# One weight load split by partitions, TensorE's two gaps filled, and a table touched early, in a decode step on one core

## The chip, the cores and the metric

The kernel runs on one core of one Trainium2 chip. The metric is the device time of one execution in microseconds, the median of several runs. The core has five engines with instruction streams of their own: TensorE (PE) for matrix products, VectorE (DVE), ScalarE (ACT), GpSimd (POOL) and SyncE (SP), which here does nothing but issue loads. Data moves between HBM and the on-chip memory (SBUF) on 16 DMA engines; a DMA that is issued once is cut into packets, and each DMA engine that takes part writes the DMA's semaphore when its own share has landed (a completion write below). Matrix products land in PSUM, eight banks of 512 fp32 values in 128 partitions.

## The reference

One decode step of a transformer block for four sequences, all tensors bf16: attention over a cached sequence of 8192 positions with 32 heads of 128, then a gated MLP.

```python
B, Sq, D = 4, 1, 512;  H, Sk, Dh = 32, 8192, 128;  F = 1792
x = A_x
q = layernorm(x) @ wq                       # per head, D x (H*Dh)
p = softmax(q . k_cache * Dh**-0.5)         # per sequence and head, 8192 scores
h = x + concat_heads(p . v_cache) @ wo
g, u = layernorm(h) @ w_gate, layernorm(h) @ w_up
out = h + (sigmoid(g) * u) @ w_down
```

The two caches are 268 MB each; everything else is about 14 MB. Every byte is read once.

## The kernel before, in words

**Units.** The 128 pairs of sequence and head are worked on four at a time: `NU` = 32 units. A unit's K (8.4 MB) and V (8.4 MB) are one load each, 64 KB in each of 128 partitions. Three slots of SBUF hold them: K alternates between slots 0 and 1, V lives in slot 2, and the last V goes to slot 0 in two halves (`vh0`, `vh1`). SP issues all loads in the order of `order`: K of the next unit, V of this one, and so on.

**A unit's work.** `unit(u)` writes, for each engine, K's 16 chunks (`k_chunk`: DVE transposes a chunk, L320, and TensorE multiplies it with the query window `Lq`, L329), then the maxima and the exponentials (`maxima`, L336 to L343), then the P times V of the unit before (`pv(u - 1)`, L368, with the fold of its four strips, L377 and L381, and `extract`, L386 and L387), then the transposed weights `PTz` of this unit (`weights`, L349). Each engine runs its list in that order; a wait on a semaphore stands in front of an operation only where data comes from another engine. Units 1 to 31 are one loop on TensorE, and after it come, outside any loop, the last unit's P times V, in two halves of 32 matmuls that wait for `vh0` and `vh1`, and its fold and extraction.

**The tail.** ACT touches the square root's table while it has nothing else (L424). TensorE multiplies the collected outputs `OT` with wo (L431, 32 matmuls in two groups of 16, each with its own half of wo) on top of x, which has been in the same bank since the start. `layernorm` (L266 to L280) normalises the sum h: statistics on DVE, a square root on ACT, the row on DVE, four small transposing matmuls into bank `XS`, a copy. ACT then copies h to SBUF (L438). TensorE multiplies with w_gate (16 matmuls) and w_up (16 matmuls, the first 12 with the first up load and the last 4 with the second), both at L446, four at a time in four strips of columns. ACT takes the sigmoid of the gate (L457), DVE multiplies and transposes in two halves (L463, L466), TensorE multiplies with w_down in 14 pairs (L471), DVE adds h (L477), and SP and ACT store half of the result each (L514).

**Loads of the tail.** When K's last chunk has been transposed, SP issues wo in two loads (L501), w_gate (L503), w_up in two loads (L507; `WUC` cuts it into three quarters and one quarter of each partition's rows), and w_down in four (L512; `WDT`). They use the slots that K and V leave. All go through SP's one queue, in this order, behind the last V halves.

**Tokens.** `prog.token(key, by)` names a count of the semaphore `key`; `prog.dma` attaches 16 to it per DMA; a wait is for the count in the token. `emit(engine, f, waits)` appends an operation to an engine's list.

Of the kernel before, what the change touches and what calls it, by code (L numbers as in the profile page):

```python
# [7 lines left out]
FP32 = mybir.dt.float32  # L8
ALU = mybir.AluOpType
ACT = mybir.ActivationFunctionType  # L10
# [3 lines left out]
class _Prog:  # L14
# [60 lines left out]
    def emit(self, eng, fn, waits=(), incs=1, ch=None):  # L75
        todo = self._waits(eng, waits)
        key = ch or eng
        tok = self.token(key, incs) if incs else None
        self._put(eng, todo, key, fn, incs, 1)
        return tok  # L80
# [40 lines left out]
def bass_sequential_preLN__mha_block_cached__glu_gated_glu__decode_kernel(  # L121
# [13 lines left out]
    _, H, S, DH = A_k_cache.shape  # L135
    F = B_w_gate.shape[1]
    assert DH == 128 and H == 32 and D == 512 and F % 128 == 0 and B == 4 and S == 8192
    NC = D // 128
# [3 lines left out]
    NU = B * H // HU  # L142
# [9 lines left out]
    WUC = (0, 3, 4)  # L152
# [3 lines left out]
    prog = _Prog({"p2d": "dve", "d2d": "dve", "a2d": "dve", "d2p": "pe", "a2p": "pe",  # L156
                  "d2a": "act", "p2a": "act",
                  "k0": "dve", "k1": "dve", "v2": "pe"})
    emit = prog.emit

    with ExitStack() as es:
        def SB(name, shape, dt):
            return es.enter_context(nc.sbuf_tensor(name, shape, dt))

        def raw(t):
            return t.tensor if hasattr(t, "tensor") else t
# [3 lines left out]
        Lq = SB("Lq", [128, 528], BF16)  # L170
# [4 lines left out]
        mask = SB("mask", [128, 8], BF16)  # L175
# [5 lines left out]
        negm = SB("negm", [128, 32], FP32)  # L181
        rsb = SB("rsb", [128, 32], FP32)
        ident = SB("ident", [128, 16], BF16)
        dummy = SB("dumm", [128, 2], FP32)
        eps = SB("eps", [128, 1], FP32)

        kTb = kT[:, :].bitcast(BF16)
# [11 lines left out]
        def reg(slot, off, size):  # L199
            return KV[:, slot * SLOT + off:slot * SLOT + off + size]  # L200
# [14 lines left out]
        bank = [PS[:, 512 * i:512 * (i + 1)] for i in range(8)]  # L215
        SBK, OBK, EX, XS, XO, QB, DN = 0, 1, 2, 3, 4, (5, 6), 7
# [12 lines left out]
        t_wg = prog.token("wg", 16)  # L229
        t_wu = [prog.token(f"wu{i}", 16) for i in range(len(WUC) - 1)]  # L230
        t_vh = [prog.token(f"vh{i}", 16) for i in range(2)]
        t_wd = [prog.token(f"wd{i}", 16) for i in range(len(WDT) - 1)]

        t_eps = emit("pool", lambda e: e.memset(eps[:, :], EPS))
# [24 lines left out]
        for b in (OBK, EX, *QB, DN):  # L259
            t_ps0 = emit("act", lambda e, b=b: e.activation(bank[b], bass.AP(raw(Lq), 0, [[528, 128], [0, 512]]), ACT.Copy), [t_lq0])  # L260

        def cols(t, c):
            return t[:, c:c + NC * (B - 1) + 1:NC]

        def layernorm(src, waits, dst):
            a = emit("dve", lambda e: e.bn_stats(bst, src), waits)  # L266
            a = emit("dve", lambda e: e.bn_aggr(agg, bst), [a])
            a = emit("act", lambda e: e.activation(std[:, 0:1], agg[:, 1:2], ACT.Sqrt, bias=eps[0:B, :]), [a, t_eps])
            a = emit("dve", lambda e: e.reciprocal(std[:, 1:2], std[:, 0:1]), [a])
            t_row = emit("dve", lambda e: e.tensor_scalar(  # L270
                row, src, agg[:, 0:1], std[:, 1:2], op0=ALU.subtract, op1=ALU.mult), [a])

            def f(e):
                ins = None
                for c in range(NC):
                    ins = e.matmul(cols(bank[XS], c), row[:, c:c + NC * 127 + 1:NC], ident[0:B, 0:B],
                                   start=(c == 0), stop=(c == NC - 1), skip_group_check=True)
                return ins
            a = emit("pe", f, [t_row, t_ident])
            return t_row, emit("dve", lambda e: e.tensor_copy(dst, bank[XS][:, 0:NC * B]), [a])  # L280
# [4 lines left out]
        _, t_xn = layernorm(x_bf, [t_x], xnT)  # L285

        t_qr = []
        for g in range(2):
            def f(e, g=g):
                made = []  # L290
                for c in range(NC):
                    for h in range(HU):
                        rhs = wq_v[:, c, 2048 * g:2048 * (g + 1)].rearrange("p (k h d) -> p h k d", k=4, h=HU)[:, h]
                        made.append(e.matmul(PS[32 * h:32 * h + B, 512 * QB[g]:512 * QB[g] + 512], cols(xnT, c), rhs,  # L294
                                             start=(c == 0), stop=(c == NC - 1), tile_position=(0, 32 * h)))
                return made[-4:]
# [9 lines left out]
        t_tr, t_sc, t_pv, t_ex, t_mx, t_exp, t_ptz, t_lq, t_ocp, t_ot, t_kd, t_vd = ({} for _ in range(12))  # L306
# [40 lines left out]
        def weights(u):  # L347
            def f(e):
# [7 lines left out]
            st_["rs"] = emit("dve", lambda e: e.transpose(  # L356
                rsb[:, :], bass.AP(raw(sgr), 0, [[1, 128], [0, 32]])), [a], ch="d2d")

        def pv(u):
            slot = slots["v", u]  # L360
            ob = 512 * OBK

            def f(e, ks):
                made = []
                for k in ks:
                    j, n, r4 = k % 4, k // 4, k % 4
                    lhsT = PTz[:, 512 * r4 + n:512 * r4 + n + 481:32]
                    made.append(e.matmul(PS[32 * j:32 * j + 16, ob:ob + 512], lhsT,  # L368
                                         KV[:, slot * SLOT + 512 * k:slot * SLOT + 512 * (k + 1)],
                                         start=(k < 4), stop=(k >= 60), tile_position=(0, 32 * j)))  # L370
                return made[-4:]
            if u < NU - 1:
                t_pv[u] = emit("pe", lambda e: f(e, range(64)), [t_ptz[u], toks["v", u], t_ps0], incs=4, ch="p2a")
            else:
                for x in range(2):
                    t_pv[u] = emit("pe", lambda e, x=x: f(e, range(32 * x, 32 * x + 32)), [t_ptz[u], t_vh[x]], incs=4, ch="p2a")
            t_ocp[u] = emit("act", lambda e: e.activation(O_sb, bank[OBK], ACT.Copy), [t_pv[u]], ch="a2p")  # L377

            def fs(e, q):
                rhs = bass.AP(O_sb.tensor, O_sb.offset + 128 * q, [[O_sb.ap[0][0], 128], [1, 4], [4, 32]])  # L380
                return e.matmul(bank[EX][:, 0:128], selw[:, q:q + 128], rhs, start=(q == 0), stop=(q == 3))  # L381
            t_vd[u] = emit("pe", lambda e: fs(e, 0), [t_ocp[u], t_selc, t_ps0, t_ot.get(u - 1)], ch="p2x")
            t_ex[u] = emit("pe", lambda e: [fs(e, q) for q in range(1, 4)][-1], ch="p2d")

        def extract(u, t=0):
            a = emit("dve", lambda e: e.transpose(OTf[:, :], bank[EX][:, 0:128]), [t_ex[u]], ch="d2d")  # L386
            t_ot[u] = emit("dve", lambda e, i: e.tensor_scalar(  # L387
                bass.AP(raw(OT), i * (4 * TU) + 4 * (u - TU * t), [[NU * 4, 128], [1, 4]]),
                OTf[:, 0:97:32], rsb[:, 1:2], None, op0=ALU.mult), [a, st_["rs"]], ch="d2p")

        def unit(u, t=0):
            for c in range(NT):
                k_chunk(u, c)
            maxima(u)
            if u + 1 < NU:
                q_window(u + 1, t)
            if u:
                pv(u - 1)
                extract(u - 1, t)
            else:  # L400
                emit("dve", lambda e: e.memset(OT[:, :, :], 0.0), ch="d2p")
            weights(u)
# [5 lines left out]
        for u in range(1, NU):  # L408
# [9 lines left out]
            if first:  # L418
                prog.end("dve", "act")
        prog.close("pe")  # L420
        pv(NU - 1)
        extract(NU - 1)

        emit("act", lambda e: e.activation(dummy[:, 0:1], mask[:, 0:1], ACT.Sqrt), [t_mask])  # L424

        for i in range(len(WOG) - 1):
# [6 lines left out]
                return ins  # L433
            t_pj = emit("pe", f, [t_wo[i], t_ot[B * WOG[i + 1] - 1]])
        t_row, t_hn = layernorm(h_ps, [t_pj], hnT)

        def f(e):
            return [e.activation(h_sb[32 * x:32 * x + B, :], h_ps[:, HD * x:HD * (x + 1)], ACT.Copy) for x in range(2)]  # L438
# [36 lines left out]
        for t in range(NFT):  # L475
# [5 lines left out]
                 tok=t_wq)  # L481
        for n, (x, u) in enumerate(order):
# [7 lines left out]
            if halves:  # L490
                for i in range(2):
# [4 lines left out]
                     tok=toks[x, u])  # L496
        k_done, v_done = t_kd[NU - 1], t_vd[NU - 2]
# [6 lines left out]
            reg(1, 16384, NC * F), B_w_gate.rearrange("(p c) f -> p (c f)", p=128)), [k_done], tok=t_wg)  # L504
        wu_src = B_w_up.rearrange("(p c) f -> p (c f)", p=128)
        for i in range(len(WUC) - 1):
            prog.dma("sp", f"wu{i}", lambda e, i=i: e.dma_start(  # L507
                reg(1, 16384 + (NC + WUC[i]) * F, (WUC[i + 1] - WUC[i]) * F), wu_src[:, WUC[i] * F:WUC[i + 1] * F]),
                     [k_done], tok=t_wu[i])
        wd_src = B_w_down.rearrange("(p t) f -> p t f", p=128)  # L510
        for i in range(len(WDT) - 1):
            prog.dma("sp", f"wd{i}", lambda e, i=i: e.dma_start(  # L512
# [53 lines left out]
```

## Time and profile before

| | |
|---|---|
| median of 3 runs | 1281.62 us (1281.55 to 1281.74) |
| the profiled execution | 1281.89 us, of which the profile's span is 1280.1 |
| TensorE products, share of the span | 62% |
| VectorE | 62% |
| ScalarE | 4% |
| bytes read | 550.77 MB, mean 430 GB/s |
| the loads' queue, share of 16 DMA engines | 99.6% |
| mean granted TensorE clock | 0.81 |

The page gives times in microseconds from the span's start. The granted clock is TensorE's, as a share of full speed; it is 1.00 or 0.50 here and changes in steps. A row of the timeline is a run of like instructions: start, busy time, engine, line, operation, operands, count, and in brackets how long the engine had been idle and what it waited for. In the chain of waits, each row is a piece of the work that ended last. In the windows, each row is a stretch of time with the busy time of each engine, the granted clock, the mean share of the DMA engines that were busy and the rate. Completion writes are read from the trace's records of the DMAs' semaphores, one per DMA engine and DMA; these records don't say which engine wrote.

### The profile page before, as it was taken

Reading aid. Unit: us, or ns where it says so; the run is one execution under the profiler, and the core shown is the slowest. Engines: PE = TensorE matmul, PEld = TensorE weight load, DVE = VectorE, ACT = ScalarE, POOL = GpSimd, SP = SyncE. Lnnn points to the kernel's source line nnn. Section 1 sums busy time; section 2 is a strip of 40 time slices with the busy share of each in tenths; the row PEclk is TensorE's granted clock in tenths of the full one; section 3 lists DMA queues with packets and bytes.
Section 4 is the critical chain, followed back from the end, with each engine's and each line's share of the span. In section 5 each row is a group of like instructions: output and inputs, shape, how many; then the busy total and the mean of one; then the engine's idle time right before and its main releaser. Section 6 shows DMA issues by size and latency. Waiting matters only on the chain. (4 is left out here: it accounts for less than half of the span.)

```text
span 1280.1 us, 10700 instructions
## 1 busy us (share of the span) xinstructions
PE 789.8 (62%) x4485; PEld 292.0 (23%) x4485; DVE 797.5 (62%) x1075; ACT 55.2 (4%) x112; POOL 4.3 (0%) x18
## 2 busy tenths in 40 slices
PE   1676755557755557655557655567655577555586
PEld 0122212222212222212222212222122222122232
DVE  1876675567675567665567665566765666755671
ACT  2000000000000000000000000000000000000001
POOL 1000000000000000000000000000000000000000
PEclk8888877788877788877788877788777888777887
DMA  9999999999999999999999999999999999999998
GB/s 420 431 425 428 451 430 428 426 442 440 426 428 432 451 426 428 428 451 430 428 426 440 442 426 428 432 451 426 428 428 448 432 428 426 440 442 426 428 426 341
DMA packets 11596, 550.83 MB, mean 430 GB/s; under 512 B 1212, under 2 KB 1224, under 8 KB 2888
## 3 DMA queue, kind: packets, MB, share of 16 engines
q1 hardware_dynamic: 11576, 550.77, 99.6%
q8 instruction: 3, 0.05, 0.0%
q10 hardware_dynamic: 16, 0.01, 0.0%
q14 instruction: 1, 0.01, 0.0%
HBM read 550.77 MB, written 0.00 MB: 430 GB/s over the span
## 5 line engine op out<-in xcount | busy, mean ns | idle before, releaser
L329 PE MATMUL PS<-kT,Lq 128*128 128x512 bf16 x2048 | 587.9, 419 | 439.0 <-DVE kT L320 420.6
L320 DVE STREAM_TRANSPOSE kT<-KV 128x1024 f32<-128x1024 f32 x512 | 612.1, 1230 | 239.5 <-DMA KV<-in_A_k_cache_dram 192.1
L329 PEld LDWEIGHTS PS<-kT,Lq 128*128 128x128 bf16 x2048 | 176.9, 104 | 848.3 <-DVE kT L320 684.4
L368 PE MATMUL PS<-KV,PTz 128*16 128x512 bf16 x2048 | 120.5, 389 | 6.7 <-DVE PTz L349 3.5
L386 DVE STREAM_TRANSPOSE kT<-PS 128x128 f32<-128x128 f32 x32 | 10.1, 317 | 161.3 <-PE PS L381 161.3
L349 DVE STREAM_TRANSPOSE PTz<-E_sb 32x512 bf16<-32x512 bf16 x128 | 89.7, 701 | 3.6 <-ACT E_sb L343 0.6
L381 PE MATMUL PS<-kT,selw 128*128 128x128 f32 x256 | 66.3, 415 | 24.9 <-ACT kT L377 24.9
L368 PEld LDWEIGHTS PS<-KV,PTz 128*16 128x16 bf16 x2048 | 59.4, 110 | 65.6 <-issue 16.4
L343 ACT ACTIVATE E_sb<-PS,negm 128x512 bf16<-128x512 f32 x32 | 22.0, 687 | 1144.5 <-DVE negm L341 1144.5
L381 PEld LDWEIGHTS PS<-kT,selw 128*128 128x128 f32 x256 | 49.8, 206 | 43.9 <-ACT kT L377 40.8
L336 DVE TENSOR_REDUCE part<-PS 128x1 f32<-128x512 f32 x32 | 22.1, 692 | 35.8 <-PE PS L329 35.8
L377 ACT ACTIVATE kT<-PS 128x512 f32<-128x512 f32 x32 | 19.1, 598 | 61.1 <-PE PS L368 61.1
L387 DVE TENSOR_SCALAR OT<-kT,rsb 128x4 f32 (+1 forms) x32 | 7.3, 229 | 4.4
L313 DVE TENSOR_TENSOR Lq<-q_all,mask 128x32 bf16<-128x32 bf16 x32 | 9.6, 301 | 0.0
L431 PE MATMUL PS<-KV,OT 128*4 128x512 bf16 x32 | 8.4, 429 | 0.0
L341 DVE STREAM_TRANSPOSE negm<-mxr 128x32 f32<-128x32 f32 x32 | 6.8, 213 | 1.1
L338 DVE STREAM_TRANSPOSE turn<-part 128x32 f32<-128x32 f32 x32 | 6.8, 211 | 1.1
L356 DVE STREAM_TRANSPOSE rsb<-sgr 128x32 f32<-128x32 f32 x32 | 6.8, 211 | 1.1
L353 DVE STREAM_TRANSPOSE turn<-part 128x32 f32<-128x32 f32 x32 | 6.8, 212 | 1.0
L294 PE MATMUL PS<-KV,kT 128*4 128x512 bf16 x32 | 3.6, 627 | 5.4 <-DMA KV<-in_A_wq_dram 5.4
L339 DVE TENSOR_SCALAR_CACHE_REDUCE turn<-turn 128x32 f32<-128x32 f32 x32 | 5.9, 186 | 1.1
L301 DVE STREAM_TRANSPOSE kT<-PS 128x512 f32<-128x512 f32 x2 | 1.4, 717 | 8.2 <-PE PS L294 8.2
(52 smaller groups left out, 54.6 us busy)
## 6 DMA issues: line engine op xcount, KB each, us to landing
KV<-in_A_v_cache_dram SPq DMA_DIRECT2D x2, 4096.0 KB, 45.3
KV<-in_A_wq_dram SPq DMA_DIRECT2D x1, 4096.0 KB, 12.5
KV<-in_A_wo_dram SPq DMA_DIRECT2D x2, 2048.0 KB, 25.2
KV<-in_B_w_gate_dram SPq DMA_DIRECT2D x1, 1792.0 KB, 31.3
KV<-in_B_w_down_dram SPq DMA_DIRECT2D x3, 512.0 KB, 21.2
KV<-in_B_w_up_dram SPq DMA_DIRECT2D x1, 1344.0 KB, 23.2
KV<-in_A_k_cache_dram SPq DMA_DIRECT2D x32, 50.1
KV<-in_A_v_cache_dram SPq DMA_DIRECT2D x31, 31.4
```

Source lines behind the costliest of these rows:

```text
L313: t_lq[u] = emit("dve", lambda e, i: e.tensor_tensor(dst, bass.AP(raw(q_all), i * (4 * TU) + 4 * (u - TU * t), [[NU * 4, 128], [1, 4], [0, ...
L320: t_tr[u, c] = emit("dve", lambda e: e.transpose(kT[:, (c % 2) * TW:(c % 2 + 1) * TW], KVw[:, o:o + TW]), w, ch="d2p")
L329: ins = e.matmul(bank[SBK], Lq[:, 128 * t + 15 - c:128 * t + 143 - c], rhs, start=(c == 0 and t == 0), stop=(c == NT - 1 and t == 3))
L336: a = emit("dve", lambda e: e.tensor_reduce(part[:, 0:1], bank[SBK], AX.X, ALU.max), [t_sc[u, NT - 1], t_pool], ch="d2d")
L343: t_exp[u] = emit("act", lambda e: e.activation(E_sb[:, :], bank[SBK], ACT.Exp, bias=negm[:, 0:1], scale=SCALE, accum_out=part[:, 1:2]), [ ...
L349: return [e.transpose(PTz[32 * q:32 * (q + 1), :].rearrange("p (r q c) -> p r q c", r=4, q=4)[:, :, q, :], E_sb[32 * q:32 * (q + 1), :].re ...
L368: made.append(e.matmul(PS[32 * j:32 * j + 16, ob:ob + 512], lhsT, KV[:, slot * SLOT + 512 * k:slot * SLOT + 512 * (k + 1)], start=(k < 4), ...
L377: t_ocp[u] = emit("act", lambda e: e.activation(O_sb, bank[OBK], ACT.Copy), [t_pv[u]], ch="a2p")
L381: return e.matmul(bank[EX][:, 0:128], selw[:, q:q + 128], rhs, start=(q == 0), stop=(q == 3))
L386: a = emit("dve", lambda e: e.transpose(OTf[:, :], bank[EX][:, 0:128]), [t_ex[u]], ch="d2d")
L387: t_ot[u] = emit("dve", lambda e, i: e.tensor_scalar(bass.AP(raw(OT), i * (4 * TU) + 4 * (u - TU * t), [[NU * 4, 128], [1, 4]]), OTf[:, 0: ...
L431: ins = e.matmul(h_ps, OT[:, B * g:B * (g + 1), j], wo_v[:, g, j, :], start=False, stop=(g == 7 and j == 3), skip_group_check=True)
```

## The change

Three edits, all behind the loop.

1. The second up load (one quarter of w_up, 3584 bytes in each of 128 partitions) becomes two DMAs, of partitions 0 to 99 and of 100 to 127, issued one after the other at the same place in SP's order. Both count on the same semaphore; a second token is drawn for it, so the wait is for 32.
2. `filler(n)` puts n matmuls of 128x512 on TensorE, from the query window `Lq` with itself, into the bank `XS`, which nothing reads before the layernorm of h overwrites it. Twelve stand in front of the last unit's P times V, eighteen between its halves. They wait for nothing that is not long there.
3. An ACT instruction with the sigmoid on one column goes behind the second layernorm, in front of the copies of h. It writes a column of `dummy` that nothing reads; `dummy` is two columns wider for it.

```diff
-        dummy = SB("dumm", [128, 2], FP32)
+        dummy = SB("dumm", [128, 4], FP32)
...
         t_vh = [prog.token(f"vh{i}", 16) for i in range(2)]
+        t_wu[-1] = prog.token(f"wu{len(WUC) - 2}", 16)
...
+        def filler(n):
+            emit("pe", lambda e: [e.matmul(bank[XS], Lq[:, 0:128], Lq[:, 0:512], start=True, stop=True) for _ in range(n)][-1],
+                 [t_ps0, t_lq[NU - 1]], incs=0)
...
                 for x in range(2):
+                    if x:
+                        filler(18)
                     t_pv[u] = emit("pe", lambda e, x=x: f(e, range(32 * x, 32 * x + 32)), [t_ptz[u], t_vh[x]], incs=4, ch="p2a")
...
         prog.close("pe")
+        filler(12)
         pv(NU - 1)
         extract(NU - 1)
...
         t_row, t_hn = layernorm(h_ps, [t_pj], hnT)
+        emit("act", lambda e: e.activation(dummy[:, 2:3], mask[:, 0:1], ACT.Sigmoid))
...
         for i in range(len(WUC) - 1):
-            prog.dma("sp", f"wu{i}", lambda e, i=i: e.dma_start(
-                reg(1, 16384 + (NC + WUC[i]) * F, (WUC[i + 1] - WUC[i]) * F), wu_src[:, WUC[i] * F:WUC[i + 1] * F]),
-                     [k_done], tok=t_wu[i])
+            for a, b in ((0, 100), (100, 128)) if i == len(WUC) - 2 else ((0, 128),):
+                prog.dma("sp", f"wu{i}", lambda e, i=i, a=a, b=b: e.dma_start(
+                    reg(1, 16384 + (NC + WUC[i]) * F, (WUC[i + 1] - WUC[i]) * F)[a:b], wu_src[a:b, WUC[i] * F:WUC[i + 1] * F]),
+                         [k_done], tok=t_wu[i])
```

## The prediction

> **What bounds the kernel now.** I read the page first, then the chain of waits, then the last microseconds in half-microsecond windows, then the timeline of the tail, then the completion writes of single DMAs.
>
> The page, DMA row of the slices and the queue row:
>
> ```profile
> span 1280.1 us, 10700 instructions
> DMA  9999999999999999999999999999999999999998
> q1 hardware_dynamic: 11576, 550.77, 99.6%
> ```
>
> The 16 DMA engines are busy from start to end: the kernel is a stream of 550.77 MB. A packet of 65536 B takes 2.42 us on one engine, so nothing but the stream's own end can move much. The chain of waits (start, us, what) says what ends last:
>
> ```profile
> 1253.74 0.42 SPq L512
> ...
> 1254.21 21.99 DMA KV<-in_B_w_down_dram
> ...
> 1276.24 1.33 PE PS L471 x12
> 1277.57 0.02 issue
> 1277.60 0.42 DVE KV L477
> ```
>
> The last matmuls wait for the third of four w_down loads (tiles 8 to 11), not for TensorE's own past. The windows (last two columns: DMA share, GB/s) show how the stream ends:
>
> ```profile
> 1273.50:1274.00 0.50, 0.00 (x0) 0.00 (x0) 0.47 (x2) 0.00 (x0) 0.00 (x0) 1.00 0.95 365
> 1274.00:1274.50 0.50, 0.20 (x4) 0.18 (x6) 0.50 (x2) 0.00 (x0) 0.00 (x0) 1.00 0.68 238
> 1274.50:1275.00 0.50, 0.41 (x10) 0.10 (x6) 0.43 (x2) 0.00 (x0) 0.00 (x0) 1.00 0.22 90
> 1275.00:1275.50 0.50, 0.50 (x8) 0.26 (x8) 0.00 (x0) 0.00 (x0) 0.00 (x0) 1.00 0.18 66
> 1275.50:1276.00 0.50, 0.09 (x2) 0.00 (x0) 0.00 (x0) 0.00 (x0) 0.00 (x0) 1.00 0.15 49
> 1276.00:1276.50 0.50, 0.26 (x6) 0.21 (x8) 0.00 (x0) 0.00 (x0) 0.00 (x0) 0.94 0.07 25
> ```
>
> Most engines are done by 1274.5, and for 2 us a few finish alone. The completion writes name them. The third w_down load completes on 13 engines at 1273.81 to 1274.30, then at 1275.22, 1275.90 and 1276.20; call these late engines L1, L2, L3. The lags (0.9, 1.6, 1.9 us behind the 13) are in every DMA since 90 us: packets of code (16384 B at 53.83 and 87.88, 8192 B at 65.87) each hit one engine and left it 1.0 to 1.55 us behind, where it stays. A fourth code packet at 1274.33 hits one of the 13, call it E: the last w_down load completes on 12 engines by 1274.92, then at 1275.85, 1276.48, 1276.53 and 1276.82. The second up load (128 packets of 3584 B, 0.140 us each, eight per engine) completes at 1269.97 to 1270.45, and on L1 to L3 at 1271.42, 1272.11 and 1272.40.
>
> The timeline of the tail:
>
> ```profile
> 1236.72 3.65 PE L368 MATMUL PS<-KV,PTz 128*16 128x512 bf16 x64
> ...
> 1246.70 3.61 PE L368 MATMUL PS<-KV,PTz 128*16 128x512 bf16 x32 [3.48 <-DVE PTz L349]
> ...
> 1253.54 3.61 PE L368 MATMUL PS<-KV,PTz 128*16 128x512 bf16 x32 [3.22 <-DMA KV<-in_A_v_cache_dram]
> ...
> 1260.03 8.41 PE L431 MATMUL PS<-KV,OT 128*4 128x512 bf16 x32
> ...
> 1271.54 1.28 ACT L457 ACT_TABLE_LOAD   x1
> ```
>
> 64 matmuls took 3.65 us at granted clock 1.00; after the gaps 32 take as long, at 0.50.
>
> **The change part by part.** The sum is made against the profiled execution, 1281.89 us (span 1280.1 and 1.8 around it). It stands 0.27 above the median, 1281.62.
>
> *Split of the up load.* Every DMA here gives equal shares: 128 rows make eight packets on each of 16 engines, the 4 rows of x four packets and four completion writes. Held to equal shares on at most 16 engines, 100 rows run on 10 engines with ten rows, 28 on 14 with two. If both count from the same end, ten engines carry 12 rows instead of 8 (+4 x 0.140 = +0.56 us), four carry 2 (-0.84) and two none (-1.12). [...] A price per row between 0.140 (all 128 packets) and 0.140 x 2.75 (the two 2048 B packets beside the last code packet took 0.23 instead of 0.084, if engines should disturb each other so) is possible; I take 0.140, the row of the same packets. The other end puts the ten at 1274.92 + 0.56 + 2.45 = 1277.9. A gain on them is excluded, as they carry more bytes.
>
> If L1, L2, L3 and E are among the six that shed rows: the third w_down load completes at 1276.20 less 0.84 to 1.12 = 1275.08 to 1275.36, the last at 1276.82 less the same = 1275.70 to 1275.98; the ten are at 1274.92 + 0.56 = 1275.48. The last six pairs of matmuls start 0.04 after the third load, and the last pair 0.86 later (now 1276.24 and 1277.10): 1275.98 to 1276.26, or two pairs after the last load, 1275.95 to 1276.23. So -0.84 to -1.12; I take -0.95.
>
> *One more DMA on SP.* 0.33 (shortest cache load) to 1.17 us (second up load) of issue. The w_down issues behind it end at 1258.64 and land 19.4 to 22.0 us later, and SP has nothing else until 1278.04: 0. With that cover gone, it would be up to 1.17.
>
> *Twelve products before the last P V.* TensorE idles 3.48 us from 1243.22. At full clock K's products of this shape follow each other every 0.218 us: 12 x 0.218 = 2.6, over at 1245.85; PTz comes at 1246.65. Cost 0, cover 0.8. The clock, which fell at 1245.7, should then stay: the first half takes 1.8 us instead of 3.6.
>
> *Eighteen between the halves.* From 1248.5, 18 x 0.218 = 3.9, over at 1252.45; the half of V they precede lands at 1253.49. Cost 0, cover 1.0. At half clock (0.427 each, as L431's first eight) they would take 7.7. The second half then takes 1.8 (-1.8), the fold (L381) 2.07 instead of 2.17, wo's first 16 products 3.5 from 1258.1 to 1261.6. There the next wait stands: the second half of wo completes at 1263.73. The other 16 run to 1267.4 instead of 1268.44: 1.05 us of some 3.4 are left.
>
> *Sigmoid's table.* The load (1.28) is moved, not added; the dummy adds 0.20 (as at L424). It sits on ACT behind the square root, now ending 1268.65, so over at 1270.13; behind it are the two copies of h (0.77, wanted only by the last addition), over at 1270.9. The gate's products, from 1270.28, end near 1271.2, the sigmoid at 1271.8. The first three quarters of up are late next: the first up load completes on L3 at 1271.32, its products and the last quarter's end at 1272.3 (now 1273.02). The multiplication starts at 1272.33 instead of 1273.41 and w_down's products at 1273.2 instead of 1274.30.
>
> By themselves the TensorE and ACT edits are worth 0: TensorE already waits (0.65 us) for the third w_down load. They keep TensorE ahead when that load comes 0.95 earlier. The sum: 1281.89 - 0.95 = 1280.9 for the profiled execution, 1280.7 on the median's level.
>
> **The rivals.** The trace doesn't number the engines, so which engines are late decides.
>
> *A late engine among the ten.* L3 there: third load at 1276.20 + 0.56, last pair 0.56 later: 1282.2. Only L2: 1275.90 + 0.56 = 1276.46, 0.26 later: 1281.9. It decides as soon as one of these two is among the ten, and ends slower than before. For it: ten of sixteen places. Against: L1 to L3 are no three independent draws; in the very first load they were already the last three (0.56 to 0.81 us behind the first, the others at most 0.43), so they look like neighbours, all in or all out. [...]
>
> *E among the ten.* The last code packet comes as TensorE starts on L471; with 60 instructions more (30 products and their weight loads) it comes earlier, near L446, and E carries 1.54 + 0.56 from there: third load 1274.30 + 2.1 = 1276.40, last pair +0.2, 1281.8. Left where it is, the last load completes at 1276.48 + 0.56 = 1277.04: the same.
>
> *The split evens out.* 100 and 28 rows spread over all 16 give seven to nine rows each, at most 0.14: 1281.6. Against it: equal shares in every DMA of the trace. [...]
>
> *Fillers at half clock.* 12 x 0.427 = 5.1 delay the first half by 1.65 to 1248.35, it ends at 1251.95, 18 x 0.427 = 7.7 end at 1259.6, 6.1 late; less 0.65 of slack and up to 1.5 if L431 is at full clock: 1285.6 to 1287. It decides from 1.0 us of overrun. [...]
>
> **How the numbers follow.** Forecast 0.42 (own range 1280.3 to 1281.0); late engine among the ten 0.22; E 0.17; evened out 0.09; half clock or ten engines that disturb each other badly 0.06; a gain over 0.2% 0.04, for which no row gives more than about 2 us. 0.2% (2.56 us) is about what a measurement of this kernel can tell from no change. The first four cases lie within it: 0.90. The range runs from the forecast's lower end, with a little for a full clock in the last products (five spacings of 0.107 instead of 0.207), to the dearer late engine: 1280.0 to 1282.4.
>
> **What would show it.** Right: 3584 B completions on 10 and 14 engines; L3's third w_down completion near 1275.2; granted clock 1.00 through 1246 to 1263; P V halves of 1.8 us; no table load between gate and sigmoid; TensorE's last wait still on w_down. Wrong: a late engine 0.56 later than now, a code packet on a loaded engine, or the second half of P V starting after 1253.6.

## The result, and the profile after

The changed kernel takes 1283.72 us (median of 20 runs, 1282.35 to 1285.01) against 1281.55 (median of 20 runs, 1280.93 to 1282.13): a ratio of 1.0016, 95% interval 1.0010 to 1.0022. It is slower, by about 2.2 us, and lies above the predicted range of 1280.0 to 1282.4. The profiled execution took 1283.67 us, of which 1282.0 are the span; before these were 1281.89 and 1280.1.

The chain of waits of the changed kernel (start, us, what):

```profile
1250.80 0.90 SPq L517
1251.69 0.04 issue
1251.73 22.88 DMA KV<-in_B_w_up_dram
1274.61 0.04 issue
1274.66 0.65 PE PS L455 x4
...
1276.30 1.87 PE PS L480 x16
1278.17 0.00 issue
1278.17 1.49 PE PS L480 x12
```

The last thing waited for was a w_down load before, and is now the second up load, the one that was split. Its last completion write comes at 1274.61; before, it came at 1272.40. The products that need it (L455, L446 before) end 2.3 us later, and everything behind them follows: w_down's products (L480) start at 1276.30 instead of 1274.30. The third w_down load, the last wait before, is level with it: its last completion write comes at 1278.12 (1276.20 before), 0.05 us before the products ahead of those that need it are through. By these rows, either delay alone would have set nearly the same end.

The timeline of the changed kernel shows that the other two edits do what the prediction said (PEld is TensorE's loading of weights):

```profile
1242.77 2.54 PE L361 MATMUL PS<-Lq 128*128 128x512 bf16 x11
...
1246.19 1.93 PE L373 MATMUL PS<-KV,PTz 128*16 128x512 bf16 x32 [0.89 <-DVE PTz L350]
...
1253.05 1.93 PE L373 MATMUL PS<-KV,PTz 128*16 128x512 bf16 x32 [0.94 <-DMA KV<-in_A_v_cache_dram]
...
1268.32 1.28 ACT L444 ACT_TABLE_LOAD   x1
...
1270.98 0.54 ACT L466 ACTIVATE KV<-PS 128x448 f32<-128x448 f32 x1 [0.51 <-PE PS L455]
...
1272.71 1.29 PE L455 MATMUL PS<-KV,kT 128*4 128x448 bf16 x12 [1.86 <-DMA KV<-in_B_w_up_dram]
...
1274.66 0.54 PE L455 MATMUL PS<-KV,kT 128*4 128x448 bf16 x4 [0.65 <-DMA KV<-in_B_w_up_dram]
...
1278.17 0.94 PEld L480 LDWEIGHTS PS<-KV 128*4 128x4 bf16 x12 [0.50 <-DMA KV<-in_B_w_down_dram]
```

The fillers (L361; 11 of the 12 and 17 of the 18 are in the trace) leave 0.9 us free ahead of either half of P times V, each half takes 1.93 us instead of 3.61, and no table load stands ahead of the sigmoid (L466), which ends at 1271.5 instead of 1273.4. And then TensorE waits 1.86 and 0.65 us for the two up loads.

The windows of the changed kernel say why (last two columns: share of the DMA engines that were busy, GB/s):

```profile
1268.00:1269.00 1.00, 0.00 (x0) 0.00 (x0) 0.63 (x2) 0.98 (x2) 0.00 (x0) 1.00 1.01 342
1269.00:1270.00 1.00, 0.36 (x8) 0.28 (x12) 0.49 (x2) 0.99 (x3) 0.00 (x0) 1.00 1.00 209
1270.00:1271.00 1.00, 0.85 (x16) 0.22 (x16) 0.00 (x0) 0.46 (x3) 0.00 (x0) 1.00 1.02 232
1271.00:1272.00 1.00, 0.00 (x0) 0.00 (x0) 0.00 (x0) 0.53 (x1) 0.00 (x0) 1.00 0.97 200
1272.00:1273.00 1.00, 0.29 (x4) 0.11 (x8) 0.00 (x0) 0.00 (x0) 0.00 (x0) 0.57 1.01 284
1273.00:1274.00 1.00, 1.00 (x12) 0.14 (x4) 0.00 (x0) 0.00 (x0) 0.00 (x0) 0.50 0.99 330
```

The same windows of the kernel before:

```profile
1269.00:1270.00 1.00, 0.00 (x0) 0.00 (x0) 0.57 (x4) 0.29 (x1) 0.00 (x0) 1.00 1.00 401
1270.00:1271.00 1.00, 0.23 (x4) 0.21 (x4) 0.71 (x1) 0.25 (x1) 0.00 (x0) 1.00 1.04 415
1271.00:1272.00 1.00, 0.73 (x18) 0.39 (x20) 0.17 (x1) 0.96 (x3) 0.00 (x0) 1.00 1.03 409
```

The DMA engines are as busy as before, and move half as much: 200 to 232 GB/s instead of some 410. Read the share and the rate together; the share alone shows nothing. The packet records say the same of single packets. The 128 packets of 3584 B took 0.140 us in the median before, and 0.253 now (0.240 in the mean). Their neighbours got slower too: those of the first up load 0.446 us in the mean instead of 0.408, and those of 4096 B after 1262 0.201 instead of 0.163. Over all three kinds that is 12.5 + 4.9 + 15.2 = 32.6 us more, or 2.0 us on each of 16 engines; 20.1 of them are the neighbours'. The 4096 B packets belong to the w_down loads (with a few of wo's), which are the same as before and go to all 128 partitions. They are slow while rows of the split load are still being written: those that start before 1272 take 0.29 to 0.33 us in the mean of each microsecond, those of 1274 to 1275 take 0.169 and later ones 0.163 at most; the last packet of the split load starts at 1273.51. In the kernel before they take 0.159 to 0.164 throughout.

### The profile page after: what moved, and what is told of

The parts are those of the page before. It is cut to its first block, busy times and chain, and to the rows that moved or that the text cites. A ratio compares the mean times of both kernels' runs of the same rounds, so it can differ in the third digit from the quotient of the medians.

```text
span 1282.0 us, 10760 instructions
## 1 busy us (share of the span) xinstructions
PE 797.3 (62%) x4513; PEld 295.3 (23%) x4515; DVE 797.1 (62%) x1075; ACT 55.3 (4%) x113; POOL 4.3 (0%) x18
## 5 line engine op out<-in xcount | busy, mean ns | idle before, releaser
L373 PE MATMUL PS<-KV,PTz 128*16 128x512 bf16 x2048 | 117.1, 381 | 1.8 <-DMA KV<-in_A_v_cache_dram 0.9
L361 PE MATMUL PS<-Lq 128*128 128x512 bf16 x28 | 6.5, 379 | 0.1
```

## The experiments

Two theories at first: the split costs the time, because its packets and their neighbours become slower; or the fillers cost it, since TensorE is at half clock for its last products (granted clock 0.50 from 1272.1 on). Then: why are the packets slower? Candidates are the unequal count of rows, a second DMA as such, the way the rows are read, and the place where they are written. Times are medians; the kernel before ran beside each (1281.40 to 1281.55). A ratio is to the kernel before, with its interval.

| kernel | us | ratio (95% interval) | packets of the second up load, median and mean us |
|---|---|---|---|
| changed | 1283.72 | 1.0016 (1.0010 to 1.0022) | 0.253, 0.240 |
| no split | 1281.48 | 0.9999 (0.9990 to 1.0008) | 0.140, 0.142 |
| split alone | 1283.22 | 1.0013 (1.0004 to 1.0022) | 0.240, 0.231 |
| halves by column | 1281.27 | 0.9998 (0.9989 to 1.0007) | 0.074, 0.076 (1792 B) |
| 64 and 64 partitions | 1284.30 | 1.0020 (1.0011 to 1.0029) | 0.269, 0.261 |
| 100 and 28, read as one block | 1283.74 | 1.0018 (1.0009 to 1.0028) | 0.245, 0.233 |
| first 64 partitions only | 1282.66 | 1.0010 (1.0001 to 1.0019) | 0.162, 0.199 |
| eight of 16 | 1283.70 | 1.0017 (1.0007 to 1.0026) | 0.241, 0.230 |
| four of 32 | 1283.93 | 1.0018 (1.0009 to 1.0028) | 0.280, 0.269 |
| 100 and 28, ahead of wo | 1283.48 | 1.0016 (1.0006 to 1.0026) | 0.233, 0.227 |
| fillers alone | 1281.52 | 1.0002 (0.9993 to 1.0011) | 0.140, 0.142 |
| no split, more fillers | 1281.04 | 0.9997 (0.9988 to 1.0006) | 0.140, 0.142 |

### The changed kernel without the split

```diff
-        t_wu[-1] = prog.token(f"wu{len(WUC) - 2}", 16)
...
-            for a, b in ((0, 100), (100, 128)) if i == len(WUC) - 2 else ((0, 128),):
+            for a, b in ((0, 128),):
```

> The changed kernel with the second up load put back into one DMA; fillers and the early sigmoid stay. Theory 1, the split costs the time because the packets of the 100-row DMA and of its neighbours become slower (0.25 us for 3584 B instead of 0.14): without it all packets of 3584 B take 0.14 again and the time is 1281.0 to 1281.6, level with the kernel before or up to 0.5 us faster, since the last w_down loads land where they did. Theory 2, the fillers cost it, by leaving TensorE at half clock for its last 44 products: 1283 or more, with the packets at 0.14.

1281.48 us, level with the kernel before. Its windows have the full rate again, while TensorE's clock is 0.50 for the last products here too:

```profile
1270.00:1271.00 1.00, 0.93 (x16) 0.29 (x16) 0.00 (x0) 0.56 (x2) 0.00 (x0) 1.00 0.99 396
1271.00:1272.00 1.00, 0.88 (x12) 0.20 (x12) 0.00 (x0) 0.54 (x1) 0.00 (x0) 0.70 1.03 410
1272.00:1273.00 1.00, 0.74 (x8) 0.09 (x4) 0.04 (x1) 0.00 (x0) 0.00 (x0) 0.50 1.04 414
```

The half clock is thus not what costs the time.

### The split alone

The kernel before, with the loop over `((0, 100), (100, 128))` and the second token, and nothing else of the change.

> The kernel before with the split alone. Theory 1: packets of 3584 B near 0.25 us, the third w_down load lands 1 to 2 us later than before, 1283.0 to 1284.5, at least as slow as the whole change. Theory 2: 1280.5 to 1281.6.

1283.22 us, 1.7 more than the kernel before. The split alone brings the loss; fillers and sigmoid bring neither loss nor gain. "At least as slow as the whole change" was expected; the 0.5 us between the two are within the intervals. The third w_down load's last completion comes at 1277.39, 1.2 us later than before.

### Two DMAs, by columns

```diff
-            for a, b in ((0, 100), (100, 128)) if i == len(WUC) - 2 else ((0, 128),):
+            n = (WUC[i + 1] - WUC[i]) * F
+            for a, b in ((0, n // 2), (n // 2, n)) if i == len(WUC) - 2 else ((0, n),):
                 prog.dma("sp", f"wu{i}", lambda e, i=i, a=a, b=b: e.dma_start(
-                    reg(1, 16384 + (NC + WUC[i]) * F, (WUC[i + 1] - WUC[i]) * F)[a:b], wu_src[a:b, WUC[i] * F:WUC[i + 1] * F]),
+                    reg(1, 16384 + (NC + WUC[i]) * F + a, b - a), wu_src[:, WUC[i] * F + a:WUC[i] * F + b]),
```

> The changed kernel, but the second up load is split by columns: two DMAs of all 128 partitions with rows of 1792 B. Theory 1 (what hurts is which partitions an engine writes): packets near 0.075 us each (the 2048 B ones take 0.084), times within 0.4 us of the one without the split. Rival, a second DMA of small packets costs by itself: about 2 us slower than the one without the split.

1281.27 us, with packets of 0.074. A second DMA costs nothing here (1281.48 with one), with all 128 partitions in each.

### Equal counts: 64 and 64 partitions

```diff
-            for a, b in ((0, 100), (100, 128)) if i == len(WUC) - 2 else ((0, 128),):
+            for a, b in ((0, 64), (64, 128)) if i == len(WUC) - 2 else ((0, 128),):
```

> The changed kernel with the split at 64: two DMAs of 64 partitions, every engine carries four rows of each, eight in all as before. If the unequal count of rows (twelve, two, none) is the cause: packets of 0.14 us and a time within 0.4 us of the one without the split. If the cause is that several engines write to neighbouring or related partitions at once: packets of 0.25 us or more although all carry the same, and 0.5 to 1.5 us slower than the one without the split. [...]

1284.30 us: 2.8 slower than without the split, more than the 0.5 to 1.5 expected, with packets of 0.269, where 0.25 or more was expected of places that several engines write at once. By equal shares each engine carries eight rows, as in the kernel before, so the unequal count is not the cause. Its windows:

```profile
1269.00:1270.00 1.00, 0.32 (x8) 0.23 (x12) 0.54 (x2) 0.99 (x3) 0.00 (x0) 0.61 1.03 179
1270.00:1271.00 1.00, 1.00 (x12) 0.35 (x16) 0.00 (x0) 0.50 (x2) 0.00 (x0) 0.50 1.06 201
1271.00:1272.00 1.00, 0.64 (x8) 0.00 (x0) 0.00 (x0) 0.23 (x1) 0.00 (x0) 0.50 0.89 146
```

### The same places, read otherwise

```diff
+                near = B_w_up.rearrange("d f -> (d f)")[a * F:b * F].rearrange("(p f) -> p f", f=F)
...
-                    reg(1, 16384 + (NC + WUC[i]) * F, (WUC[i + 1] - WUC[i]) * F)[a:b], wu_src[a:b, WUC[i] * F:WUC[i + 1] * F]),
+                    reg(1, 16384 + (NC + WUC[i]) * F, (WUC[i + 1] - WUC[i]) * F)[a:b],
+                    near if i == len(WUC) - 2 else wu_src[a:b, WUC[i] * F:WUC[i + 1] * F]),
```

> The changed kernel, but the two DMAs of the second up load read one contiguous block of HBM (row after row) instead of a quarter of every fourth row; the same bytes go to the same partitions on the same engines, so that a quarter of w_up is wrong. If the packets are slow because of how the 100 rows are read: 0.14 us again and near 1281.5. If they are slow because of where they are written: still about 0.25 us, 1283 to 1284.5.

1283.74 us and 0.245 us a packet: how the rows lie in HBM doesn't matter here. (The split load reads every fourth row of w_up whole, 3584 B, and not a quarter of it.) Of the four candidates, the place where the rows are written is left.

### Half the bytes

The changed kernel without the split, with `((0, 64),)` for the second up load.

> The changed kernel with one DMA for the second up load and of its first 64 partitions alone: the other half isn't loaded, 229 KB less, so that a quarter of up is wrong in half its rows. If an engine's own packets are all that counts: 64 packets at 0.14 us, four per engine instead of eight, 0.56 us less on each, about 0.5 us faster than with the whole load in one DMA (1281.48). If the place written limits, with half of the places sharing all writes: packets near 0.27 us, four per engine take as long as eight do at 0.14, the same time within 0.3 us or slower, although half the bytes are gone.

1282.66 us, 1.2 slower than the whole load in one DMA, although half the bytes are gone. "Within 0.3 us or slower" holds; that it would be so much slower was not expected, and the price of a packet missed: 0.162 us in the median (0.199 in the mean), not 0.27. The loss is the neighbours': its own 64 packets take 12.7 us in all, against 18.2 for the 128 of the whole load, but the 4096 B packets after 1262 take 0.201 us in the mean, as in the changed kernel. The windows of this kernel dip just where those 64 packets and their neighbours run:

```profile
1269.00:1270.00 1.00, 0.29 (x4) 0.21 (x4) 0.61 (x2) 0.99 (x3) 0.00 (x0) 1.00 1.10 209
1270.00:1271.00 1.00, 0.90 (x16) 0.30 (x16) 0.04 (x1) 0.62 (x2) 0.00 (x0) 0.76 0.95 325
1271.00:1272.00 1.00, 0.39 (x7) 0.00 (x0) 0.00 (x0) 0.49 (x1) 0.00 (x0) 0.50 1.08 293
1272.00:1273.00 1.00, 0.92 (x12) 0.24 (x12) 0.00 (x0) 0.05 (x1) 0.00 (x0) 0.50 0.96 282
```

### How fine are the places? Four of 32, eight of 16

```diff
-        t_wu[-1] = prog.token(f"wu{len(WUC) - 2}", 16)
+        for _ in range(3):
+            t_wu[-1] = prog.token(f"wu{len(WUC) - 2}", 16)
...
+            for a, b in [(p, p + 32) for p in range(0, 128, 32)] if i == len(WUC) - 2 else ((0, 128),):
```

That is the version with 32 partitions. The one with 16 draws seven tokens more, and its parts are 16 partitions each.

> The changed kernel with the second up load in four DMAs of 32 partitions, two rows per engine and DMA. [...] If places are only neighbours, 32 partitions are half as many as 64 and the packets near 0.4 to 0.56 us, 1285 to 1287.

> The changed kernel with the second up load in eight DMAs of 16 partitions, one row per engine and DMA, eight rows per engine in all. [...] If the slow packets come of two DMAs side by side, or of sharing as such, they stay near 0.27 us and the time near 1284.3. [...]

32 partitions behave like 64 (0.280 against 0.269 us, 1283.93 against 1284.30), not as expected of half as many places (0.4 to 0.56 us). And 16 partitions are no worse (0.241 us, 1283.70): the result lies near what was expected if sharing as such makes the packets slow, however many places are shared. A possible reason is that the engines don't run abreast. The completion writes of one DMA are spread over 0.5 us, plus 1 to 2 us for the late engines, and a row takes a quarter of a microsecond, so several of the eight DMAs are under way at once and together reach more places. That is an argument and was not measured; how many engines meet at one place at a time stays open.

### Is it the wait or the stream?

The changed kernel with the split load issued ahead of wo (`up_load(i)` issues up load i just as in the changed kernel):

```diff
+        up_load(1)
         wo_src = A_wo.rearrange("(g p j) f -> p g (j f)", p=128, j=4)
...
+        up_load(0)
```

> The changed kernel with the split second up load issued ahead of wo instead of behind the first up load, so that nothing waits for it for 20 us. If the loss is that the up products wait for the late load (they end at 1275.3 in the changed kernel), it is gone: 1281.3 to 1281.7. If the loss is in the stream itself, since the DMA engines move less while they disturb each other, everything behind lands later all the same: packets of 3584 B and the wo packets beside them slow, the third w_down load 1 to 2 us later than before, 1282.7 to 1284.

1283.48 us. Nothing waits for the split load now, and the loss is the same. The rate dips 18 us earlier (the kernel before has 373, 406 and 410 GB/s in these windows):

```profile
1252.00:1253.00 1.00, 0.40 (x2) 0.00 (x0) 0.00 (x0) 0.00 (x0) 0.00 (x0) 1.00 0.85 193
1253.00:1254.00 1.00, 0.00 (x0) 0.00 (x0) 0.00 (x0) 0.00 (x0) 0.00 (x0) 1.00 1.03 221
1254.00:1255.00 1.00, 0.00 (x0) 0.00 (x0) 0.00 (x0) 0.00 (x0) 0.00 (x0) 1.00 0.92 222
```

and all loads behind land later: the third w_down load completes on 12 engines at 1276.37 to 1276.94, where 13 did so by 1274.30 before. wo's last 16 products wait for their load until 1266.09, where they start at 1263.42 in the changed kernel. So the loss is in the stream: the bytes that weren't moved in those microseconds come later.

### Fillers alone

The kernel before with `filler` and its two calls.

> The kernel before with the thirty unread products alone; one DMA for the second up load, the sigmoid's table loaded where it was. Theory (TensorE's gain ends at the third w_down load): 1281.2 to 1281.6, no change. Rival (the fillers gain, and something in the early sigmoid gives it back): below 1281.1.

1281.52 us: no change that can be measured, as forecast.

### Which engines are late

```diff
+        t_pr = [prog.dma("sp", f"pr{n}", lambda e, n=n, i=i: e.dma_start(
+            probe[0:n, 4 * i:4 * (i + 1)], B_w_gate[0:n, 0:4]), [k_done]) for i, n in enumerate((2, 4, 6, 8, 10, 12, 14))]
```

> The kernel before with seven tiny loads of 2, 4, 6, 8, 10, 12 and 14 rows of 8 B between wo and w_gate; nobody reads them. A load of n rows should show n completion writes, on the same n engines each time plus two more at the next, so that the one whose completions first hold a late engine (over 0.8 us behind the others) tells that engine's place. Forecast of the prediction: no late completion in the loads of 2 to 10 rows, late ones in those of 12 and 14 or in none (engines 15 and 16 in the count). Rival: a late engine among the first ten.

A single execution, 1281.63 us, so it tells of this execution alone. The load of n rows has n completion writes, plus one from the issuing side. With two rows both come at 1261.77 and 1261.81. With four, one is late (1263.06, the others by 1262.01). With six, one more comes 0.5 us behind the rest (1262.73); it follows a code packet of 8192 B at 1256.37 that the kernel before did not have in its profile. With 8, 10 and 12 rows no new one is late. With 14, two more are (1263.08 and 1263.69). So, if each load takes the engines of the one before and two more (the late ones, 0, 1, 2, 2, 2, 2 and 4, agree; the trace doesn't number the engines), one late engine is the third or fourth, and two are the 13th and 14th. The forecast had all of them behind the tenth.

### A version with more fillers

```diff
+        filler(8)
         t_row, t_hn = layernorm(h_ps, [t_pj], hnT)
...
+        filler(4)
         t_hh = []
...
         for t in range(NFT):
+            if t == 8:
+                filler(3)
```

on top of the kernel without the split.

> The changed kernel with one DMA for the second up load, and more unread products: eight behind wo's products, four behind up's, three ahead of w_down's ninth pair. Theory: with the packets normal, the end is set by the third w_down load plus TensorE's last twelve products, 1.49 us at half clock and 0.65 at full; kept at full clock they give 0.3 to 0.6 us, 1280.9 to 1281.2. Rival: the clock falls anyway, or the fourth w_down load ends last: 1281.3 to 1281.6.

1281.04 us (1280.88 to 1281.50), against 1281.45 for the kernel before beside it (1280.99 to 1281.98). It lies where the theory put it, but the interval of the ratio reaches from 0.9988 to 1.0006, so that it beats the kernel before isn't shown. That the clock stays up is. Its last windows are at full clock:

```profile
1275.00:1276.00 1.00, 0.84 (x10) 0.42 (x11) 0.00 (x0) 0.00 (x0) 0.00 (x0) 1.00 0.16 59
1276.00:1277.00 1.00, 0.69 (x10) 0.10 (x6) 0.24 (x1) 0.00 (x0) 0.00 (x0) 1.00 0.00 0
```

and its last twelve products take 0.99 us instead of 1.49 in the changed kernel. They don't reach the 0.65 of the theory, because the last four wait for the fourth w_down load (its last completion comes at 1276.27), which was part of the rival. The third w_down load ends at 1275.63 here, and at 1275.82 to 1276.20 in the other profiles in which no load is cut by partitions: differences of half a microsecond between single profiles are no effect of an edit.

## Why the prediction was wrong

**The step that failed: the price of a row, and of the rows beside it.** The prediction took 0.140 us for each of the ten engines' rows, "the row of the same packets". It named the other end itself (0.140 x 2.75, "if engines should disturb each other so") and left it to a case of 0.06 together with half clock. The packets took 0.253 in the median, 1.8 times as much. With that price the prediction's own term for the ten engines, twelve rows less eight, is 12 x 0.253 - 8 x 0.140 = 1.92 us instead of 0.56. (Its other end, 1277.9, made only ten of the twelve rows dearer; with all twelve it is 1278.4.) The row of 0.140 was a bad witness: all 128 packets behind it belong to a load of all 128 partitions. There was no load in the trace, beside four rows of x, that goes to fewer partitions, and so no row for the case at hand.

**What the sum put at nothing.** Even at 2.75 times, only the ten engines' own rows were made dearer. The runs show the neighbours slow as well: the end of the first up load, and the w_down loads that follow while some engines still write rows of the split. They carry 20.1 of the 32.6 us of packet time that the change adds. The late engines lose much of their time ahead of their own rows of the split: from the completion of w_gate to that of the first up load they take 4.6 to 5.0 us, taken in order, against 3.25 to 3.29 before. With 64 partitions and equal counts the same happens, with half the bytes too, and with another way of reading no less. So count, source and a second DMA as such are excluded. What is left is which partitions the engines write while others write too. That is shown by elimination and by the neighbours' times; what it is that collides was not measured.

**Shares of rows.** Right in their number: the split load has 24 completion writes from the data side, as many as 10 and 14 make (both parts count on one semaphore, so the two are seen only as their sum). That both parts count from the same end, from which the forecast has its twelve, two and no rows, was the author's assumption; no run shows it by itself, since the records don't say which engine wrote.

**The late engines.** Half right. Four engines are late in the changed kernel: after a packet of code at 1259.46 there is one more than before. The first up load completes on them at 1271.85 to 1272.67, on the others by 1269.79. The last two completion writes of the split load, 1274.28 and 1274.61, come from a single engine, since fifteen have the next load, the first of w_down, by 1274.25. It has a share in both parts, so it is a late engine among the ten, and it ends the third w_down load last of all, at 1278.12. The other three late ones shed rows, as forecast, and arrive with the bulk (1276.28 to 1276.78). Three engines are ahead of all others, at 1275.16, 1275.22 and 1275.48. That is where the prediction looked for L3, but these are engines without a lag that shed rows: they had the first w_down load by 1272.36, when the late ones were at most 0.5 us past the up load before it, and the eight packets of 4096 B that each engine has of the w_down load take 1.0 to 1.3 us.

The probes agree, by the same order of the engines: of three that carry a lag before the tail, two are the 13th and 14th, and one is the third or fourth, among the ten. So "all in or all out" was wrong. No engine has such a lag from the start: in the loads of the kernel before that end ahead of the first packet of code, at 53.83, the last completion write is 0.2 us behind the next, and the lags come with packets of code, on three engines and then on a fourth. The rival "a late engine among the ten" was most likely at work too, which alone would have given 1281.9 to 1282.2 at 0.140 us a row. (That the one charged in the changed kernel is the fourth, E, isn't excluded.) In the profile the other fifteen have the third w_down load by 1276.78, 0.6 us later than its last completion before, and the charged one needs 1.3 us more. How much of the 2.2 us it would cost without the dearer rows can't be told from these runs; equal counts without any shedding lose 2.2 to 2.8 us.

**One more DMA on SP.** Right, 0: the last w_down issue ends at 1257.81, and SP is next wanted at 1280.12.

**Fillers and sigmoid.** Right in their places and in their worth, which was put at nothing by themselves. The second half of P times V waits for V as before, wo's second half stops the gain (in the kernel without the split its products start at 1263.54; forecast 1263.77), and alone they give nothing that can be measured. Two details missed. The clock was at half speed once more, from 1258.5 to 1261.9, which the wait for wo hid. And the code packet came at 1259.46, 15 us earlier than before, where some 4 us were forecast.

**The chances.** 0.90 stood on "within 0.2%", and the ratio of 1.0016 is within; its interval reaches 1.0022. The forecast of a gain inside that band was wrong, and so was the range: its upper end took in the dearer late engine at 0.140 us a row, and neither the dearer row nor the dearer neighbours. That the time stayed within 0.2% is luck: the dearer rows had no time of their own and shared a chance of 0.06.

## What to carry to other kernels

In a stream that keeps all DMA engines busy, a load cut by partitions halved the rate here, its neighbours' included (200 to 232 GB/s instead of some 410); cutting the same load by columns cost nothing (1281.27 us, against 1281.48 uncut). When a DMA-bound kernel loses time with the engines as busy as before, look at the rate and at the time of single packets. A price taken from rows that never met the condition at issue is a guess, and belongs into the range with both ends.

## What the runs showed of the hardware

Loading half of the partitions (229 KB instead of 459) made the kernel 1.2 us slower than loading all. The load cut by partitions, into parts of 64, 32 or 16 or of 100 and 28, has packets of 3584 B of 0.23 to 0.28 us in the median, against 0.140 in one load of 128 partitions; a single load of 64 has 0.162 (0.199 in the mean). Packets of unchanged loads that run at the same time get slower too (with 64 and 64 partitions, those of 4096 B that start from 1271 to 1272 take 0.413 us in the mean, against 0.163 in the kernel before). In the kernel before each of three packets of code (8192 or 16384 B, by 88 us) was followed by one more engine that is 1.0 to 1.55 us later than it was; the three lags are still there in the last loads, over 1100 us on, and set their end.
